# The first block of a convolution and MLP kernel: taps of two channel thirds on TensorE, zero products in front, loads reordered

## The chip, the cores and the metric

One core of one Trainium2 chip runs the whole program. The metric is the device time of one execution in microseconds, as the median of several executions; profiles come from the hardware profiler. Engines: PE is TensorE (PEld its weight loads), DVE is VectorE, ACT is ScalarE, POOL is GpSimd, SP is SyncE, which here only issues DMA transfers.

## The reference

```python
# x: (8, 4096, 192), weight: (8 heads, 7 taps), w_in: (192, 2048), w_out: (2048, 192)
w = softmax(weight, axis=-1)                      # 7 taps for each group of 24 channels
out[b, s, c] = sum(w[head(c), k] * x_pad[b, s + k, c] for k in range(7))   # causal, 6 zeros in front
h = out.reshape(32768, 192) @ w_in
return (h * sigmoid(h)) @ w_out                   # (32768, 192)
```

The weights come as 64-bit floats; the kernel makes 32-bit floats of them on the chip, with integer operations ("rounding").

## The kernel before

The kernel works through 32 blocks of 1024 tokens. A block is laid out as two halves of 512 tokens: channels are cut into three thirds of 64, and a tile has the 64 channels of the first half in partitions 0 to 63 and those of the second half in partitions 64 to 127. From the second block on, everything is pipelined by a hand-made plan and PE never pauses. The first block is special: it has to wait for loads, taps and rounded weights. These are its parts:

```python
def turn_in(b, k):                 # third k of x: transpose on DVE, nat -> xt (6 columns of pad in front)
    nc.vector.transpose(xt[:, k, pad : pad + TB], nats[b][:, k])

def conv(b, k, i):                 # tap i of third k; result in place of nat
    if i == 0 and b < 2:           # first tap on ACT
        nc.scalar.activation(dst, src, AF.Copy, scale=tap)
    ...
    else:                          # taps 1..6 on DVE: dst = src * tap + dst
        nc.vector.scalar_tensor_tensor(out=dst, in0=src, scalar=tap, in1=dst, op0=ALU.mult, op1=ALU.add)

def spread(b, k):                  # copy each half's 64 rows into both partition halves, by DMA
    for n in range(2):
        for e in range(2):
            nc.sync.dma_start(out=dups[b][R * e : R * e + R, n, k, :], in_=src[R * n : R * n + R, :])

def round_in(j, k=None):           # 64-bit words of w_in -> wr[j]: 8 to 10 operations on DVE and ACT
    ...

def up_plain(b, j):                # h = out @ w_in for 1/4 of the hidden units: 24 products of 64 rows, then SiLU
    ...                            # 8 PSUM banks; for j = 0 in the order of the thirds

for k in range(NK):                # the front of the first block
    if k == 0:
        turn_in(0, 0)
        conv(0, 0, 0)
    for i in range(1, K):
        conv(0, k, i)
    spread(0, k)
    if k < NK - 1:
        for j in ((1, 2), (3,))[k]:
            load_in(j, nc.sync)    # raw 64-bit weights
        turn_in(0, k + 1)
        conv(0, k + 1, 0)
    round_in(0, k)
round_in(1)
for j in range(NJ):
    up_plain(0, j)
    ...                            # rounding of the other weights
```

Each product of 32-bit floats is two instructions on PE. Products are written into the 8 PSUM banks (`ps` in the views); `bank()` takes one of them. `pin` keeps an instruction in program order. SiLU is h * sigmoid(h). In what follows, "j=1" is the second call of `up_plain`: 48 instructions, followed by 96 for j=2 and j=3.

Of the kernel before, what the change touches and what calls it, by code (L numbers as in the profile page):

```python
# [9 lines left out]
F32 = mybir.dt.float32  # L10
I32 = mybir.dt.int32
AF = mybir.ActivationFunctionType
ALU = mybir.AluOpType
# [4 lines left out]
def kernel(  # L18
# [24 lines left out]
    nc = tc.nc  # L43
# [3 lines left out]
    H, K = weight.shape  # L47
    NT = B * S
    DFF = moe_w_in.shape[1]
    P = 128  # L50
    R = 64
    NK = D // R
    grp = D // H
    pad = K - 1
    TB = 512
# [14 lines left out]
    xpool = ctx.enter_context(tc.tile_pool(name="xp", bufs=1))  # L70
    tpool = ctx.enter_context(tc.tile_pool(name="tp", bufs=3))
    gpool = ctx.enter_context(tc.tile_pool(name="gp", bufs=2 * NJ))
    upool = ctx.enter_context(tc.tile_pool(name="up", bufs=13))
# [29 lines left out]
    def pin(ins):  # L103
        return tc.keep_in_program_order(ins)
# [8 lines left out]
    vec, act = Pinned(nc.vector), Pinned(nc.scalar)  # L113

    def bank():
        return psum.tile([P, TB], F32, tag="ps", name="ps")

    nats, xts, gs = {}, {}, {}

    def load(b, ks=range(NK)):  # L120
        if b not in nats:
            nats[b] = xpool.tile([P, NK, TB // SQ, SQ], F32, tag="nat", name="nat")
        nat = nats[b]
        for k in ks:
            for i in range(P // SQ):
                c = R * k + SQ * (i % 2)
                (nc.sync if b or k or i % 2 else nc.scalar).dma_start(  # L127
                    out=nat[SQ * i : SQ * i + SQ, k, :, :],
                    in_=x_v[2 * b + i // 2][:, :, c : c + SQ],
                )  # L130


    wexp = const.tile([P, H, K], F32, name="wexp")
    nc.scalar.dma_start(
        out=wexp.rearrange("p h k -> p (h k)"),
        in_=weight.rearrange("(o h) k -> o (h k)", o=1).to_broadcast([P, H * K]),
# [5 lines left out]
    for k in range(NK):  # L142
        nc.gpsimd.dma_start(
            out=xts[0][R:P, k, 0:pad], in_=x0[:, k, :], allow_slow_non_contiguous=True
        )
    load(0, (0,))

    warm = const.tile([P, 1], F32, name="warm")
    vec.memset(warm, 0.0)
    act.activation(warm, warm, AF.Exp)  # L150


    WC = 2 * NK * P
# [2 lines left out]
    wr = [const.tile([P, 2, NK, P], F32, name=f"wr{j}") for j in range(NJ)]  # L156
# [5 lines left out]
    def raw_tile(key):  # L162

        pool, tag = (gpool, "g") if key in (("i", 2), ("i", 3)) else (tpool, "t")
        raws[key] = pool.tile([P, 4 * TB], I32, tag=tag, name="raw")[:, 0 : 2 * WC]
        return raws[key]

    def load_in(j, queue):
        raw = raw_tile(("i", j)).rearrange("p (a k c) -> p a k c", a=2, k=NK)
        for e in range(2):  # L170
            for a in range(2):
                c = 2 * P * (NM * a + 2 * j + e)
                queue.dma_start(
                    out=raw[R * e : R * e + R, a, :, :], in_=in32[:, :, c : c + 2 * P]
                )
# [53 lines left out]
    def round_in(j, k=None):  # L229

        words = raws["i", j].rearrange("p (a k c t) -> p a k c t", a=2, k=NK, t=2)
        if k is None:
            rounded(
                wr[j].rearrange("p a k c -> p a (k c)"),
                words.rearrange("p a k c t -> p a (k c) t"),
                j < 2,
            )
        else:
            rounded(wr[j][:, :, k, :], words[:, :, k], j < 2)
        if k in (None, NK - 1):  # L240

            del raws["i", j]
            for e in range(2):
                nc.gpsimd.dma_start(
                    out=ws[j][R * e : R * e + R], in_=wr[j][R - R * e : 2 * R - R * e]
                )
# [33 lines left out]
        comb(a_(1, 0), a_(0, 0), a_(1, 0), ALU.subtract)  # L280

    load_in(0, nc.sync)
    load(0, (1, 2))


    hot = const.tile([P, NK, H], F32, name="hot")
    nc.gpsimd.memset(hot, 1.0)
    for e in range(2):
        half = hot[R * e : R * e + R]
        for sign, base in ((1, 0), (-1, grp - 1)):  # L290
            nc.gpsimd.affine_select(
                out=half,
                in_=half,
                compare_op=ALU.is_ge,
                fill=0.0,
                base=base,
                pattern=[[sign * R, NK], [-sign * grp, H]],
                channel_multiplier=sign,
            )
    wred = const.tile([P, H], F32, name="wred")  # L300
    taps = const.tile([P, NK, K], F32, name="taps")
    each = const.tile([P, NK, K, H], F32, name="each")

    def per_head(t):
        return t.unsqueeze(2).to_broadcast([P, H, K])

    vec.tensor_reduce(wred, wexp, axis=AX.X, op=ALU.max)
    vec.tensor_tensor(wexp, wexp, per_head(wred), op=ALU.subtract)
    act.activation(wexp, wexp, AF.Exp)
    vec.tensor_reduce(wred, wexp, axis=AX.X, op=ALU.add)  # L310
    vec.tensor_scalar(wred, wred, scalar1=1e-9, scalar2=None, op0=ALU.add)
    vec.reciprocal(wred, wred)
# [12 lines left out]
    def turn_in(b, k):  # L325
        if k == 0 and b:
            xt = xts[b] = xpool.tile([P, NK, pad + TB], F32, tag="xt", name="xt")
            if b * TT % S == 0:
                nc.gpsimd.memset(xt[0:R, :, 0:pad], 0.0)
            else:  # L330
                nc.gpsimd.tensor_copy(xt[0:R, :, 0:pad], tails.pop(b))
        xt = xts[b]
        pin(
            nc.vector.transpose(  # L334
                xt[:, k, pad : pad + TB], nats[b][:, k, :, :].rearrange("p k c -> p (k c)")
            )
        )
        if k == NK - 1:
            if b:
                nc.sync.dma_start(out=xt[R:P, :, 0:pad], in_=xt[0:R, :, TB : TB + pad])  # L340
            if (b + 1) * TT % S:
                tails[b + 1] = xpool.tile([R, NK, pad], F32, tag="tail", name="tail", bufs=2)
                nc.sync.dma_start(out=tails[b + 1], in_=xt[R:P, :, TB : TB + pad])

    def conv(b, k, i):

        src = xts[b][:, k, i : i + TB]
        dst = nats[b][:, k, :, :].rearrange("p k c -> p (k c)")
        tap = taps[:, k, i : i + 1]
        if i == 0 and b < 2:  # L350
            pin(nc.scalar.activation(dst, src, AF.Copy, scale=tap))  # L351
        elif i == 0:
            pin(nc.vector.tensor_scalar(dst, src, scalar1=tap, scalar2=None, op0=ALU.mult))
        else:
            pin(
                nc.vector.scalar_tensor_tensor(  # L356
                    out=dst, in0=src, scalar=tap, in1=dst, op0=ALU.mult, op1=ALU.add
                )
            )

    def spread(b, k):

        if k == 0:
            dups[b] = xpool.tile([P, 2, NK, TB], F32, tag="dup", name="dup")
        src = nats[b][:, k, :, :].rearrange("p k c -> p (k c)")
        for n in range(2):
            for e in range(2):
                nc.sync.dma_start(
                    out=dups[b][R * e : R * e + R, n, k, :], in_=src[R * n : R * n + R, :]
                )  # L370

    dups, wins = {}, {}
# [15 lines left out]
    def rows(t, e):  # L388
        return t[R * e : R * e + R]

    def g_tile(b, j, a):
        if (b, j, a) not in gs:
            gs[b, j, a] = gpool.tile([P, 2, 2, TB], F32, tag="g", name="g")
        return gs[b, j, a]

    def up_plain(b, j):

        d = dups[b]
        outs = [(a, n) for a in range(2) for n in range(2)]
        hs = {(a, n, e): bank() for a, n in outs for e in range(2)}  # L400
        order = [(k, o) for k in range(NK) for o in outs]
        if j:
            order = [(k, o) for o in outs for k in range(NK)]
        for k, (a, n) in order:
            for e in range(2):
                nc.tensor.matmul(  # L406
                    hs[a, n, e],
                    rows(wr[j], e)[:, a, k, :],
                    rows(d, e)[:, n, k, :],
                    start=k == 0,  # L410
                    stop=k == NK - 1,
                )
            if k == NK - 1:
                for e in range(2):
                    g = g_tile(b, j, a)
                    act.activation(g[:, n, e, :], hs[a, n, e], AF.Silu)
# [229 lines left out]
    def begin_down(b):  # L646
        did.add((b, "down"))
        for k in range(NK):
            if b + 1 < NB and (b, f"v.{k}{K - 1}") in did:
                spread(b + 1, k)  # L650
# [82 lines left out]
            store(2, cols)  # L733


    for k in range(NK):
        if k == 0:
            turn_in(0, 0)
            conv(0, 0, 0)
        for i in range(1, K):  # L740
            conv(0, k, i)
        spread(0, k)
        if k < NK - 1:
            for j in ((1, 2), (3,))[k]:
                load_in(j, nc.sync)
            turn_in(0, k + 1)
            conv(0, k + 1, 0)
        round_in(0, k)
    round_in(1)
    for j in range(NJ):  # L750
        up_plain(0, j)
# [71 lines left out]
```

## Time and profile before

| | before |
|---|---|
| median, lowest to highest, us | 2418.23, 2418.12 to 2418.29 (3 runs) |
| span of the profile, us | 2416.3 |
| PE busy | 2388.7 us (99%), 17808 instructions |
| DVE busy | 2073.4 us (86%) |
| start of j=1, after PE's last wait | 37.67 us |

A busy share of 99% doesn't say where the other 1% is. The timeline of PE does: a line of it gives start, duration, engine, source line, operation, tiles and count, and in brackets how long the engine stood idle before and what released it. The prediction shows these lines and reads them.

### The profile page before, as it was taken

Reading aid. Unit: us, or ns where it says so; the run is one execution under the profiler, and the core shown is the slowest. Engines: PE = TensorE matmul, PEld = TensorE weight load, DVE = VectorE, ACT = ScalarE, POOL = GpSimd, SP = SyncE. Lnnn points to the kernel's source line nnn. Section 1 sums busy time; section 2 is a strip of 40 time slices with the busy share of each in tenths; the row PEclk is TensorE's granted clock in tenths of the full one; section 3 lists DMA queues with packets and bytes.
Section 4 is the critical chain, followed back from the end, with each engine's and each line's share of the span. In section 5 each row is a group of like instructions: output and inputs, shape, how many; then the busy total and the mean of one; then the engine's idle time right before and its main releaser. Section 6 shows DMA issues by size and latency. Waiting matters only on the chain.

```text
span 2416.3 us, 43191 instructions
## 1 busy us (share of the span) xinstructions
PE 2388.7 (99%) x17808; PEld 939.4 (39%) x17808; DVE 2073.4 (86%) x2823; ACT 989.4 (41%) x1856; POOL 68.2 (3%) x96
## 2 busy tenths in 40 slices
PE   6999999999999999999999999999999999999998
PEld 3334433334433344333443333443334433334333
DVE  8889888898888888888988889888888888898876
ACT  3234533345433345333454334543334533345432
POOL 3300000000000000000000000000000000000000
PEclk9999999999999999999999999999999999999999
DMA  8321222222222212222222222122221222222220
GB/s 157 75 45 37 39 45 53 43 43 39 36 53 50 43 32 40 50 53 40 40 36 44 53 44 47 35 36 53 53 41 34 42 45 54 41 40 43 38 40 14
DMA packets 454085, 111.65 MB, mean 46 GB/s; under 512 B 423936, under 2 KB 429056, under 8 KB 453888
## 3 DMA queue, kind: packets, MB, share of 16 engines
q1 hardware_dynamic: 450064, 106.89, 23.8%
q8 instruction: 139, 2.28, 0.4%
q0 software_dynamic: 480, 1.58, 0.3%
q10 hardware_dynamic: 3344, 0.42, 0.1%
q14 instruction: 58, 0.48, 0.1%
HBM read 31.49 MB, written 25.17 MB: 23 GB/s over the span
## 4 chain that ended last, share of the span: by engine, by line
PE 98%; DVE 1%; DMA 0%; ACT 0%; SPq 0%; issue 0%; ACTq 0%; DVEq 0%
PE ps L442 49%; PE ps L515 46%; PE ps L544 2%; PE ps L406 1%; DMA nat<-in_x_dram 0%; DVE nat L356 0%; DMA tail<-xt 0%; SPq L127 0%; DVE two L111 0%; ACT two L111 0%; ACT g L111 0%; DVE cmb L111 0%; DVE xt L334 0%; ACT u L111 0%; ACT nat L351 0%
## 5 line engine op out<-in xcount | busy, mean ns | idle before, releaser
L442 PE MATMUL ps<-dup,ws 64*128 64x512 f32 x2480 | 869.9, 589 | 0.0
L515 PE MATMUL ps<-g,wo 128*32 128x512 f32 x2976 | 661.8, 593 | 0.0
L466 DVE TENSOR_TENSOR g<-u,ps 128x512 f32<-128x512 f32 x744 | 485.5, 679 | 119.2 <-PE ps L442 90.0
L442 PE MATMUL ps<-win,wr 64*128 64x512 f32 x1488 | 567.7, 589 | 0.0
L515 PE MATMUL ps<-t,wo 128*32 128x128 f32 (+2 forms) x4528 | 500.6, 446 | 0.0
L463 ACT ACTIVATE g<-g 128x512 f32<-128x512 f32 x744 | 444.6, 631 | 97.3 <-DVE g L466 97.3
L442 PEld LDWEIGHTS ps<-dup,ws 64*128 64x128 f32 x2480 | 363.0, 187 | 292.0 <-issue 277.9
L515 PE MATMUL ps<-t,wx 128*32 128x512 f32 x2976 | 452.7, 592 | 0.0
L356 DVE SCALAR_TENSOR_TENSOR nat<-xt,taps,nat 128x512 f32<-128x512 f32 x576 | 432.0, 750 | 18.7 <-ACT nat L351 3.8
L442 PE MATMUL ps<-dup,wr 64*128 64x512 f32 x992 | 419.9, 596 | 0.0
L457 ACT COPY u<-ps 128x512 f32<-128x512 f32 x496 | 277.8, 588 | 229.1 <-PE ps L442 226.1
L583 ACT COPY cmb<-ps 96x512 f32<-96x512 f32 x30 | 17.4, 581 | 805.5 <-PE ps L515 805.5
L483 DVE TENSOR_TENSOR t<-g 128x1024 f32<-128x1024 f32 x248 | 299.6, 1219 | 27.3 <-PE ps L515 27.3
L483 DVE TENSOR_TENSOR t<-g,t 128x1024 f32<-128x1024 f32 x248 | 303.3, 1223 | 13.6 <-PE ps L515 3.2
L442 PEld LDWEIGHTS ps<-win,wr 64*128 64x128 f32 x1488 | 233.4, 187 | 175.5 <-issue 147.2
L515 PEld LDWEIGHTS ps<-t,wo 128*32 128x32 f32 x4528 | 180.3, 110 | 219.8 <-issue 199.5
L442 PE MATMUL ps<-win,ws 64*128 64x512 f32 x496 | 242.2, 589 | 0.0
L515 PE MATMUL ps<-g,wx 128*32 128x512 f32 x1488 | 234.5, 592 | 0.0
L515 PEld LDWEIGHTS ps<-t,wx 128*32 128x32 f32 x2976 | 121.9, 110 | 278.8 <-issue 269.5
L595 DVE TENSOR_TENSOR cmb<-cmb,ps 96x512 f32<-96x512 f32 x150 | 102.3, 682 | 135.2 <-ACT u L580 133.1
L442 PEld LDWEIGHTS ps<-dup,wr 64*128 64x128 f32 x992 | 160.5, 187 | 128.2 <-issue 114.3
L515 PEld LDWEIGHTS ps<-g,wo 128*32 128x32 f32 x2976 | 168.5, 110 | 98.3 <-issue 98.3
(59 smaller groups left out, 1205.4 us busy)
## 6 DMA issues: line engine op xcount, KB each, us to landing
dup<-nat SPq DMA_DIRECT2D x384, 128.0 KB, 2.3
nat<-in_x_dram SPq DMA_DIRECT2D x382, 64.0 KB, 2.4
out_dram<-osb SPq DMA_DIRECT2D x376, 64.0 KB, 2.0
raw<-in_moe_w_in_dram SPq DMA_DIRECT2D x16, 192.0 KB, 5.6
raw<-in_moe_w_out_dram SPq DMA_DIRECT2D x8, 384.0 KB, 3.9
ws<-wr POOLq DMA_DIRECT2D x8, 192.0 KB, 3.2
xt<-xt SPq DMA_DIRECT2D x31, 4.5 KB, 1.9
tail<-xt SPq DMA_DIRECT2D x24, 4.5 KB, 1.9
```

Of the source, the lines that this page charges most:

```text
L356: nc.vector.scalar_tensor_tensor(out=dst, in0=src, scalar=tap, in1=dst, op0=ALU.mult, op1=ALU.add)
L406: nc.tensor.matmul(hs[a, n, e], rows(wr[j], e)[:, a, k, :], rows(d, e)[:, n, k, :], start=k == 0, stop=k == NK - 1,)
L442: nc.tensor.matmul(bk[b, m, bn], rows(w, half), rows(v, half), start=first, stop=True, skip_group_check=True,)
L457: pin(copy(u, bk[b, m, "1"]))
L463: pin(nc.scalar.activation(g, g, AF.Silu))
L466: pin(nc.vector.tensor_tensor(g, us.pop((b, m, i)), bk[b, m, bn], op=ALU.add))
L483: pin(nc.vector.tensor_tensor(t[i // 2][:, i % 2, :], u, v, op=ALU.subtract))
L515: nc.tensor.matmul(accs[b][at][SQ * q : SQ * q + SQ, to], lhs[:, e, SQ * k : SQ * k + SQ], rhs[:, e, ts(q, TB // 4) if i == 5 else to], st ...
L544: nc.tensor.matmul(acc[k][R * n : R * n + R, :], wo[j][:, a, e, R * k : R * k + R], gs[b, j, a][:, n, e, :], start=j == 0 and a == 0 and e ...
L583: pin(nc.scalar.copy(c[0], acc[0][0:n, :]))
L595: pin(nc.vector.tensor_tensor(out_, u, v, op=ALU.add))
```

## The change

The intent is to take two of the three thirds' taps off DVE and give them to PE, which idles before j=1. A tap is a product with a diagonal matrix that holds the tap of each channel. Written as a 64x128 matrix with the diagonal twice, the product writes its result into both partition halves, so the copies by DMA (`spread`) go too. Four products of zeros in front are to raise PE's clock in time. The loads of the first block are kept in program order, with one of them on ACT's queue. The core of the diff, with cuts marked:

```diff
-                (nc.sync if b or k or i % 2 else nc.scalar).dma_start(
+                queue = nc.scalar if not b and (k == 0 and i % 2 == 0 or k == 1 and i == 0) else nc.sync
+                ins = queue.dma_start(
...
+                if not b:
+                    pin(ins)
...
+    zeros = upool.tile([P, TB], F32, tag="u", name="zeros")
+    vec.memset(zeros, 0.0)
+    idle = bank()
+    for _ in range(4):
+        pin(nc.tensor.matmul(idle, zeros[:, 0:P], zeros, start=True, stop=True))
...
     load_in(0, nc.sync)
-    load(0, (1, 2))
...
     act.activation(wexp, wexp, AF.Exp)
+    load(0, (1, 2))
...
-    for k in range(NK):
-        ...                                   (the loop shown above)
+    def diagonal(k):
+        for i in range(K):
+            act.activation(diag[:, k, i, :], one_hot, AF.Copy, scale=taps[:, k, i : i + 1])
+
+    def conv_pe(k):
+        by_pe[k] = [bank() for _ in range(2)]
+        for i in range(K):
+            for n in range(2):
+                pin(nc.tensor.matmul(by_pe[k][n], rows(diag, n)[:, k, i, :],
+                                     rows(xts[0], n)[:, k, i : i + TB], start=i == 0, stop=i == K - 1))
+
+    turn_in(0, 0)
+    diagonal(0)
+    conv_pe(0)
+    round_in(0, 0)
+    diagonal(1)
+    turn_in(0, 1)
+    conv_pe(1)
+    for j in (1, 2):
+        load_in(j, nc.sync)
+    turn_in(0, 2)
+    conv(0, 2, 0)
+    for n in range(2):
+        act.copy(dups[0][:, n, 0, :], by_pe[0][n])
+    for i in range(1, K):
+        conv(0, 2, i)
+    spread(0, 2)
+    load_in(3, nc.sync)
+    round_in(0, 1)
+    for n in range(2):
+        act.copy(dups[0][:, n, 1, :], by_pe[1][n])
+    round_in(0, 2)
     round_in(1)
```

POOL makes `one_hot`, the double identity, in five more instructions.

More of the change, by code (lines that the diff above doesn't have):

```diff
@@ L299 @@
             )
+    one_hot = upool.tile([P, TB], F32, tag="u", name="one_hot")[:, 0:P]
+    nc.gpsimd.memset(one_hot, 1.0)
+    for e in range(2):
+        half = one_hot[R * e : R * e + R].rearrange("p (a c) -> p a c", a=2)
+        for sign in (1, -1):
+            nc.gpsimd.affine_select(
+                out=half,
+                in_=half,
+                compare_op=ALU.is_ge,
+                fill=0.0,
+                base=0,
+                pattern=[[0, 2], [-sign, R]],
+                channel_multiplier=sign,
+            )
     wred = const.tile([P, H], F32, name="wred")
@@ L361, in spread @@
     def spread(b, k):
-        if k == 0:
+        if b not in dups:
             dups[b] = xpool.tile([P, 2, NK, TB], F32, tag="dup", name="dup")
@@ L405, in up_plain @@
             for e in range(2):
-                nc.tensor.matmul(
-                    hs[a, n, e],
-                    rows(wr[j], e)[:, a, k, :],
-                    rows(d, e)[:, n, k, :],
-                    start=k == 0,
-                    stop=k == NK - 1,
+                pin(
+                    nc.tensor.matmul(
+                        hs[a, n, e],
+                        rows(wr[j], e)[:, a, k, :],
+                        rows(d, e)[:, n, k, :],
+                        start=k == 0,
+                        stop=k == NK - 1,
+                    )
                 )
@@ L733, in finish @@
             store(2, cols)
-    for k in range(NK):
-        if k == 0:
-            turn_in(0, 0)
-            conv(0, 0, 0)
-        for i in range(1, K):
-            conv(0, k, i)
-        spread(0, k)
-        if k < NK - 1:
-            for j in ((1, 2), (3,))[k]:
-                load_in(j, nc.sync)
-            turn_in(0, k + 1)
-            conv(0, k + 1, 0)
-        round_in(0, k)
+    diag = gpool.tile([P, NK - 1, K, P], F32, tag="g", name="diag")
+    dups[0] = xpool.tile([P, 2, NK, TB], F32, tag="dup", name="dup")
+    by_pe = {}
+    def diagonal(k):
[5 more added lines that the diff above has]
+            for n in range(2):
+                pin(
+                    nc.tensor.matmul(
+                        by_pe[k][n],
+                        rows(diag, n)[:, k, i, :],
+                        rows(xts[0], n)[:, k, i : i + TB],
+                        start=i == 0,
+                        stop=i == K - 1,
+                    )
+                )
+    turn_in(0, 0)
[19 more added lines that the diff above has]
+    round_in(0, 2)
     round_in(1)
```

## The prediction

> **What bounds the kernel now.** I read the page first. Its strip of 40 slices shows PE at 9 in every slice but the first, at a granted clock of 9 tenths throughout. The chain that ended last is 98% PE.
>
> ```profile
> PE 2388.7 (99%) x17808; PEld 939.4 (39%) x17808; DVE 2073.4 (86%) x2823; ACT 989.4 (41%) x1856; POOL 68.2 (3%) x96
> ...
> PE   6999999999999999999999999999999999999998
> ...
> PE 98%; DVE 1%; DMA 0%; ACT 0%; SPq 0%; issue 0%; ACTq 0%; DVEq 0%
> ```
>
> The reader is to see that 2416.3 - 2388.7 = 27.6 us is all the idle time PE has, and that it can only lie at the front. So I asked for the timeline of PE, and for the chain in order of time.
>
> ```profile
> 16.59 6.29 PE L406 MATMUL ps<-dup,wr 64*128 64x512 f32 x16 [16.59 <-DVE wr L111]
> 27.01 10.15 PE L406 MATMUL ps<-dup,wr 64*128 64x512 f32 x32 [4.14 <-DMA dup<-nat]
> 37.67 31.17 PE L406 MATMUL ps<-dup,wr 64*128 64x512 f32 x144 [0.51 <-ACT g L111]
> ```
>
> ```profile
> 37.64 0.03 issue
> 37.67 31.17 PE ps L406 x144
> 68.84 41.35 PE ps L544 x192
> ```
>
> From 37.67 us on, PE never waits again for anything of weight: 16.6 + 4.1 + 0.5 = 21.2 us of its 27.6 us idle lie before. The time of the kernel is thus **37.7 us of front plus 2378.6 us of gapless PE**. Only the moment at which the second group of weights (j=1, 144 instructions for j=1 to 3) can start matters. The DVE timeline tells what sets it.
>
> ```profile
> 6.90 0.70 DVE L334 STREAM_TRANSPOSE xt<-nat 128x512 f32<-128x512 f32 x1
> 8.45 4.69 DVE L356 SCALAR_TENSOR_TENSOR nat<-xt,taps,nat 128x512 f32<-128x512 f32 x6 [0.84 <-ACT nat L351]
> 13.05 0.70 DVE L334 STREAM_TRANSPOSE xt<-nat 128x512 f32<-128x512 f32 x1
> 13.68 0.45 DVE L111 TENSOR_SCALAR two<-raw 128x256 int32<-128x256 int32 x2
> ...
> 16.45 4.68 DVE L356 SCALAR_TENSOR_TENSOR nat<-xt,taps,nat 128x512 f32<-128x512 f32 x6
> ...
> 24.45 4.68 DVE L356 SCALAR_TENSOR_TENSOR nat<-xt,taps,nat 128x512 f32<-128x512 f32 x6
> 29.05 0.49 DVE L111 TENSOR_SCALAR two<-raw 128x256 int32<-128x256 int32 x2
> ...
> 31.62 1.02 DVE L111 TENSOR_SCALAR two<-raw 128x768 int32<-128x768 int32 x2
> ...
> 36.43 1.09 DVE L111 SCALAR_TENSOR_TENSOR wr<-mh,two 128x768 f32<-128x768 f32 x1
> ```
>
> DVE works without a pause from 8.45 to 37.52 us: three thirds of taps (6 x 0.767 = 4.60 us each from start to start), three transposes, three roundings of the weights of j=0, one rounding of j=1. The last line ends at 36.43 + 1.09 = 37.52 us and writes the weights that j=1 reads; PE starts 0.15 us later. **DVE bounds the front, PE all the rest.**
>
> **What the Trainium skill says.** (1) "TensorE: Matmul & The Clock Gate", Part 1: the array runs at half clock until a free-running window of about 3.4 us has been busy, and falls back after an idle one. The trace agrees: the granted clock is 0.50 in the window of 27 to 28 us, at the start of a burst at 27.01, and full from about 32.0 us, 5.0 us later; the pitch of PE's pairs is 0.85 us before and 0.43 us after. (2) The same page, Part 3: matmuls on different row groups run at the same time. The trace agrees: two 64-row instructions of about 590 ns each retire every 0.43 us. (3) "FP8 and Floating Point Precision", TensorE Precision Notes: a true FP32 product takes four passes. The trace has two instructions for each matmul of the program, at 0.43 us for a pair of halves, so 0.86 us for two matmuls of 512 columns. (4) "DMA: Bandwidth & Descriptors", Queues, rings and completion order: an engine serves its queues in turn, packet by packet. So a load moved to the ACT queue gets ahead of SP's backlog and takes share from it; the trace before can't show that for this load.
>
> **The change, part by part.**
>
> Removed: on DVE 12 of the 18 tap instructions of the first block, 2 x 4.60 = 9.2 us. On ACT two of three first taps (0.72 us each). On SP eight of the twelve copies dup<-nat, about 2.4 us of issue per third and some 2 to 3 us to landing.
>
> Added on PE: 4 matmuls of zeros = 8 instructions, at 0.85 us cold and 0.43 us warm; started at about 1.4 us (after the memset, DVE's first work being at 0.89) they end between 6.5 and 8.2 us, depending on when the clock rises. Then per third 7 taps x 2 halves = 14 matmuls = 28 instructions, two at a time: 14 x 0.43 = 6.0 us, 12 us for both. They write both partition halves, so no dup copies are needed.
>
> Added on ACT: 14 diagonals of 128x128. ACT durations here are 0.20 us for 1 column, 0.25 for 56, 0.40 for 256, 0.72 for 512, so I estimate 0.3 us, 2.1 us per third. The first is ready soon after the taps (6.99 us), and PE eats one per 0.86 us, so they don't hold it. Four copies out of PSUM of 0.59 us each. On POOL the one-hot mask: four selects of 0.23 us grow to perhaps 0.4 us, ending at about 6.9 us, just in time.
>
> Moved: rounding of the first third of j=0 comes right after the first transpose on DVE, and taps remain only for the third third. DVE's order is now: transpose 0, round (0,0), transpose 1, transpose 2, taps of third 2, round (0,1), round (0,2), round j=1. I walk along it:
> - Transpose 0 at 6.90, as before, ended 7.6. Round (0,0) needs the raw weights. The last of their four loads was issued at 4.26 us:
>
> ```profile
> raw<-in_moe_w_in_dram SPq DMA_DIRECT2D x1, 192.0 KB, 6.5
> ```
>
>  so it landed at 10.76 us. That was hidden before (first used at 13.68) and isn't now. With a little lost to the load on the ACT queue I take 11.0. **DVE idles 3.4 us.**
> - Round (0,0): 2.57 us (as 29.05 to 31.62, without a wait for ACT), to 13.6. Transposes at 0.63 us pitch: transpose 2 starts at 14.2. Its data is the last of x to land; before, the next to last landed at 10.78 + 2.23 = 13.01, so it should be there.
> - First tap on ACT and the handover: 1.55 us from transpose to DVE's first tap (6.90 to 8.45): 15.75. Taps 4.60: 20.35. Round (0,1) 2.57: 22.9. Round (0,2) 2.57: 25.5. Round j=1 31.62 to 37.52 = 5.9: **31.4 us**.
>
> PE in parallel: taps 0 from about 7.7 or 8.2 to 14.2; taps 1 from 14.3 (transposed third at about 14.25) to 20.3; products of j=0, third 0, 8 pair slots = 3.4 us, its last two banks being freed by the copies of taps 1, which ACT makes behind the work for round (0,1), at about 22.8: done at 23.6; thirds 1 and 2 (weights at 22.9 and 25.5) 6.9 us: 30.5. ACT then has the j=1 rounding (to about 28.1), the table load of 1.28 us and SiLU from about 29.4, so banks are free in time. PE is ready about 1 us before DVE's weights. Start of j=1: about 31.5 instead of 37.67, **6.1 us earlier**.
>
> Behind it, DVE's rounding of j=2, j=3 and the output weights is one chain with the same durations, so it moves along by the same 6.1 us, and the waits of PE on it remain covered as before (weights of j=2 at 45.6 for a need at about 48). 2418.2 - 6.1 = **2412.1 us**.
>
> **Rivals.**
> (a) All 9.2 us arrive: 2409. Against it: the raw weights at 10.8 and the x loads at 13 us are walls that the order of DVE now runs into. If the raw loads land at 10 instead of 11, I get 2411.
> (b) PE becomes the bound of the front. If zeros don't warm the clock, or it drops again in a gap, the first taps run at 0.85 us a pair for some 3.4 to 5 us, and PE's slack of 1 us turns into 1 to 2 us lost: j=1 starts at 32.5 to 33.5, 2413 to 2414. For it: the first burst before ran 5.2 us at half pace. Against: the zeros come from 1.4 us on, long enough for a whole window.
> (c) Loads: if the reordered x and weight loads delay the raw weights to 13 us, DVE loses 2 us more: 2414. Total bytes up to there don't change, and the strip of DMA is nearly full from 4 to 10 us, so a shift to one side is possible.
> (d) Nothing is gained since the front was hidden: excluded by PE's 21.2 us idle before 37.67 us. A loss of 2% would be 48 us, more than the whole front.
>
> **Range and chances.** 2412.1 us from the walk; (a) gives the low end 2409.8, (b) and (c) together the high end 2415.2. All of this is 0.1 to 0.4% of the time, so within 2% is all but sure.
>
> **What would show it.** Right: a DVE timeline with idle time before the first rounding, released by the raw loads at about 11 us; six tap instructions left before 40 us; PE busy from about 1.5 us, full clock by 8.2 us; PE's last start after a wait at about 31.5 us with DVE's j=1 weights as releaser; from there to the end 2378.6 us as before. Wrong: if PE waits there for something else (ACT's SiLU, banks), if the clock is 0.5 during the tap matmuls, if the raw weights land elsewhere than 10 to 12 us, or if the stretch behind the front changes its length, for example because diag takes a g buffer and later tiles wait for it.

## The result, and the profile after

| | before | after |
|---|---|---|
| median of 6 runs each, us | 2418.11 | 2411.68 |
| lowest to highest, us | 2417.96 to 2418.29 | 2411.53 to 2412.07 |
| span of the profile, us | 2416.3 | 2410.0 |
| DVE's weights of j=1 ready, us | 37.52 | 31.23 |
| start of j=1, us | 37.67 | 31.38 |
| from there to PE's last end, us | 2372.29 | 2372.29 |
| from PE's last end to the end of the span, us | 6.36 | 6.29 |

The kernel is 6.43 us faster. The ratio is 0.9974 (95% interval 0.9961 to 0.9986): a small change, but the interval leaves out 1. Of the 6.43 us, the profile has 6.29 in the front. The long middle has the same length to a hundredth.

The timeline of PE in the changed kernel:

```profile
1.57 5.81 PE L159 MATMUL ps<-zeros 128*128 128x512 f32 x8 [1.57 <-DVE zeros L111]
8.04 12.59 PE L776 MATMUL ps<-xt,diag 64*128 64x512 f32 x56 [0.67 <-DVE xt L358]
20.44 10.50 PE L431 MATMUL ps<-dup,wr 64*128 64x512 f32 x48
31.38 31.17 PE L431 MATMUL ps<-dup,wr 64*128 64x512 f32 x144 [0.44 <-DVE wr L111]
```

PE now works from 1.57 us on. The taps of two thirds (56 instructions) took 12.59 us, and the 48 instructions of j=0 follow without a gap, at full clock. Then PE waits 0.44 us for DVE's rounded weights, its last wait; the 31.17 us of the 144 instructions behind it are those of before. The timeline of DVE:

```profile
7.20 0.70 DVE L358 STREAM_TRANSPOSE xt<-nat 128x512 f32<-128x512 f32 x1
10.93 0.49 DVE L111 TENSOR_SCALAR two<-raw 128x256 int32<-128x256 int32 x2 [3.03 <-DMA nat<-in_x_dram]
...
13.51 1.30 DVE L358 STREAM_TRANSPOSE xt<-nat 128x512 f32<-128x512 f32 x2
15.59 4.69 DVE L380 SCALAR_TENSOR_TENSOR nat<-xt,taps,nat 128x512 f32<-128x512 f32 x6 [0.79 <-ACT nat L375]
20.20 0.49 DVE L111 TENSOR_SCALAR two<-raw 128x256 int32<-128x256 int32 x2
...
30.27 0.96 DVE L111 SCALAR_TENSOR_TENSOR wr<-mh,two 128x768 f32<-128x768 f32 x1
```

DVE stands idle for 3.03 us before its first rounding: the raw weights aren't there yet. The bracket blames a load of x (`nat`), though the instruction reads `raw`. The chain of waits of the same kernel names the load of the weights:

```profile
5.18 5.67 DMA raw<-in_moe_w_in_dram
...
10.93 0.51 DVE two L111 x2
```

It was issued at 5.18 us and landed at 10.85, 5.67 us later. Where two views differ in the releaser, the operand that the instruction reads decides; loads of both kinds landed around that time.

The same care is due with PE's line of the kernel before, whose bracket at 37.67 us names ACT's SiLU (`g`) and not DVE's weights. In the eight runs in which PE waits before j=1 (before, after, e2, e3, e6, e8, e11, e12), j=1 starts 0.15 us after DVE's weights, whichever of the two is named. In the kernel before, the fourth SiLU ended just ahead of PE's start, at 37.63 us; in the changed kernel the fourth ended at 31.48, after PE had started at 31.38. So PE doesn't wait for that one, and the weights are what ends the wait.

DVE's budget closes with these lines. Before, it started its first taps at 8.45 us and needed 29.07 us to the weights of j=1. Now it starts its first rounding at 10.93 and needs 20.30. That is 8.77 us shorter and 2.48 us later, 6.29 us in all.

### The profile page after: what moved, and what is told of

It is laid out like the page before. It is cut to its first block, busy times and chain, and to the rows that moved or that the text cites. A ratio compares the mean times of both kernels' runs of the same rounds, so it can differ in the third digit from the quotient of the medians. Undisturbed runs are those within 1.5% of the kernel's fastest.

```text
span 2410.0 us, 43319 instructions
## 1 busy us (share of the span) xinstructions
PE 2401.0 (100%) x17872; PEld 943.9 (39%) x17872; DVE 2063.0 (86%) x2812; ACT 995.0 (41%) x1872; POOL 72.6 (3%) x101
## 4 chain that ended last, share of the span: by engine, by line
PE 98%; DVE 1%; DMA 0%; ACT 0%; issue 0%; SPq 0%; ACTq 0%; DVEq 0%
PE ps L468 49%; PE ps L541 47%; PE ps L570 2%; PE ps L431 1%; DVE two L111 0%; DMA raw<-in_moe_w_in_dram 0%; DVE nat L380 0%; DMA wexp<-in_weight_dram 0%; DVE mh L111 0%; DVE cmb L111 0%; DVE wr L111 0%; ACT two L111 0%; ACT u L111 0%; DVE osb L111 0%; DVE xt L358 0%
## 5 line engine op out<-in xcount | busy, mean ns | idle before, releaser
L380 DVE SCALAR_TENSOR_TENSOR nat<-xt,taps,nat 128x512 f32<-128x512 f32 x564 | 423.5, 751 | 18.3 <-ACT nat L375 3.7
```

## The experiments

Times differ by fractions of a microsecond here, so each run was read in the trace first: by the start of j=1 and by PE's last end. In every run below, 2372.2 to 2372.5 us lie between the two. What comes behind PE's last end, the final stores, took 5.88 to 7.53 us from run to run. So the measured times are blunter than the trace, by up to about a microsecond. There is one profile for each kernel; how much of the spread of the other timed runs lies there isn't shown.

| run | start of j=1 | DVE's weights of j=1 | behind PE's end | median time |
|---|---|---|---|---|
| before | 37.67 | 37.52 | 6.36 | 2418.11 |
| after | 31.38 | 31.23 | 6.29 | 2411.68 |
| e1_no_zeros | 31.75 | 31.26 | 6.29 | 2412.47 |
| e2_loads_only | 38.10 | 37.95 | 5.88 | 2417.51 |
| e3_pe_short | 31.43 | 31.28 | 6.29 | 2412.79 |
| e4_dve_short | 30.90 | 29.58 | 7.25 | 2412.02 |
| e5_both_short | 29.86 | 28.87 | 7.30 | 2411.16 |
| e6_one_third | 35.09 | 34.95 | 7.03 | 2416.36 |
| e7_three_thirds | 36.71 | 32.42 | 6.07 | 2416.98 |
| e8_hide_tap | 31.55 | 31.41 | 6.33 | 2412.05 |
| e9_early_weights | 37.04 | 35.74 | 5.96 | 2416.96 |
| e10_shared_third | 37.07 | 35.76 | 5.90 | 2416.42 |
| e11_kept_warm | 29.05 | 28.91 | 7.53 | 2410.24 |
| e12_zeros_only | 37.74 | 37.59 | 6.39 | 2418.29 |

The runs were made in three sessions; the kernel before had medians of 2418.18, 2418.21 and 2418.09 us in them. Theory: two chains run side by side in the front, DVE's to the weights of j=1 and PE's through taps and j=0, and the later one sets the time. Rivals: the loads or the zeros made the gain; DVE alone counts; PE alone counts.

### Shorter work on one chain, on the other, on both

e3 (wrong result): PE does four of the seven taps.

```diff
-        for i in range(K):
+        for i in range(0, K, 2):
             for n in range(2):
                 pin(nc.tensor.matmul(by_pe[k][n], ...
```

> Wrong result on purpose: PE does only taps 0, 2, 4, 6 of each third it has, 3 x 0.86 = 2.6 us less per third, 5.2 us less in all. DVE is as in the changed kernel. Theory (DVE's chain to the weights of j=1 bounds the front): j=1 still starts at 31.2 to 31.4, 2411.5 to 2411.8. Rival (PE's chain bounds): j=1 up to 5 us earlier, 2406.5.

```profile
14.41 5.40 PE L776 MATMUL ps<-xt,diag 64*128 64x512 f32 x16 [2.97 <-ACT diag L111]
31.43 31.17 PE L431 MATMUL ps<-dup,wr 64*128 64x512 f32 x144 [0.92 <-DVE wr L111]
```

Measured: j=1 at 31.43, DVE's weights at 31.28. PE had 5.2 us less to do and gained nothing by it. **DVE's chain bounds the changed kernel's front.** The test is milder than its edit looks: PE had to wait 2.97 us for the second group's diagonals and then ran it slowly (see e5), so it ended j=0 at 30.50 us instead of 30.94, only 0.44 us earlier. PE's wait for the weights grew by about as much, to 0.92 us, and j=1 didn't move with PE. The median of 2412.79 us is even higher; the trace shows no change of the front that would explain it, and its profiled run took 2411.95.

e4 (wrong): DVE does three instead of six taps of the last third.

```diff
-    for i in range(1, K):
+    for i in range(2, K, 2):
         conv(0, 2, i)
```

> Wrong result on purpose: DVE does three instead of six tap instructions of the third that it kept, 3 x 0.767 = 2.3 us less. PE is as in the changed kernel. Theory: DVE's weights of j=1 come at 28.9 us, but PE ends j=0 only at 30.9, so PE takes over as the bound and only 0.3 to 0.45 us are gained: j=1 at about 30.95, 2411.2. Rival (only DVE matters): all 2.3 us, j=1 at 29.1, 2409.4.

```profile
20.60 41.40 PE L431 MATMUL ps<-dup,wr 64*128 64x512 f32 x192
```

Measured: weights at 29.58, j=1 at 30.90 with PE working without a wait before it. DVE came 1.65 us earlier, not 2.3: its rounding of the last third waited 0.64 us for a step on ACT, which stood behind the copies of PE's second group of taps, so the two chains are not quite independent. Of the 1.65 us, 0.48 arrived at the start of j=1. So PE's chain stands right behind DVE's, as the trace of the changed kernel says by its wait of 0.44 us. The time doesn't show it: in the profiled run the stores behind PE's end took 7.25 us, 0.96 us more than in the changed kernel.

e5 (wrong): both edits.

> Wrong result on purpose: both shortenings at once. Theory: with PE out of the way DVE's 2.3 us come through whole: j=1 at about 29.1, 2409.4. If something third (loads, ACT's SiLU, banks) stands right behind both, less than 1 us is gained over the changed kernel: 2410.7 or more.

Measured: weights at 28.87, but j=1 only at 29.86: 1.52 us gained of 2.3. The expectation missed, and neither chain as I had drawn it explains it. The timeline of PE in this run tells why:

```profile
7.75 3.70 PE L776 MATMUL ps<-xt,diag 64*128 64x512 f32 x16 [0.53 <-DVE xt L358]
14.36 5.40 PE L776 MATMUL ps<-xt,diag 64*128 64x512 f32 x16 [2.90 <-ACT diag L111]
19.56 41.40 PE L431 MATMUL ps<-dup,wr 64*128 64x512 f32 x192
```

The same 16 instructions took 3.70 us the first time and 5.40 the second. Between them PE idled for 2.90 us. The view of stretches has the granted clock behind the busy times (it is the last number but two):

```profile
14.40:15.70 1.30, 1.30 (x6) 0.70 (x8) 0.51 (x2) 0.84 (x2) 0.00 (x0) 1.00 1.10 214
15.80:19.10 3.30, 3.30 (x11) 1.49 (x9) 3.15 (x8) 1.58 (x4) 0.00 (x0) 0.50 1.13 205
```

The clock fell to 0.50 at 15.8 us, 1.4 us after PE had gone back to work, and stayed there to 19.2. From 14.36 us on PE has no wait, so here it was the slowed PE that bounded. So e11 fills the gap with three more products of zeros.

```diff
     turn_in(0, 1)
+    idle2 = bank()
+    for _ in range(3):
+        pin(nc.tensor.matmul(idle2, zeros[:, 0:P], zeros, start=True, stop=True))
     conv_pe(1)
```

> Wrong result on purpose. Both shortenings at once, as before, with three products of zeros (2.6 us) in the gap of 2.9 us that let PE's clock fall to 0.5 from 15.8 to 19.2 us. Theory (the cold clock ate what was missing): clock 1.0 throughout, PE's second tap group 3.4 to 3.7 us instead of 5.4, DVE's weights bound again: j=1 at about 29.0 instead of 29.86. Rival (something else holds PE): j=1 at 29.8 again.

```profile
14.40 3.70 PE L776 MATMUL ps<-xt,diag 64*128 64x512 f32 x16
17.93 10.47 PE L431 MATMUL ps<-dup,wr 64*128 64x512 f32 x48
29.05 31.17 PE L431 MATMUL ps<-dup,wr 64*128 64x512 f32 x144 [0.65 <-DVE wr L111]
```

Measured: 3.70 us for the second group, and j=1 at 29.05 with DVE's weights as the releaser. All 2.33 us of DVE's saving arrive. The cold clock was what was missing in e5.

### The parts other than the taps

e2: the kernel before with the changed loads alone (of the diff above, the lines of the queue, `pin(ins)` and the moved `load(0, (1, 2))`).

> The kernel before with nothing but the changed loads of the first block (pinned order, one load of the second third on the ACT queue, issued behind the first activation). Theory: DVE bounds the front, and its first taps cover these loads, so the weights of j=1 still come at 37.5 us and j=1 starts at 37.7: 2418.2, no gain (within 0.4). Rival: the loads are where the gain is: up to several us faster, j=1 well before 37 us.

Measured: j=1 at 38.10, 0.43 us later than before. In the profiled run the stores at the end took 0.48 us less and made up for that: its span is 2416.3 us, as before. The median of the four timed runs was 0.7 us lower; no trace here shows why, as the profiled run was the slowest of them (2417.98). Nothing of the 6.3 us in the front comes from the loads.

e12: the kernel before with the four zero products alone.

> The kernel before with nothing but the four products of zeros in front. Theory: they warm a clock that falls again before the first real product at 16.6 us, and PE isn't the bound there: j=1 at 37.7, 2418.2, no gain. Rival (the zeros alone bring part of the gain): 1 us or more faster.

Measured: j=1 at 37.74; no gain. The clock was full from 5.36 us on, and back at 0.5 at 12.19, long before the first real product at 16.68.

e1: the changed kernel without the zero products.

```diff
-    for _ in range(4):
-        pin(nc.tensor.matmul(idle, zeros[:, 0:P], zeros, start=True, stop=True))
```

> The changed kernel without the four products of zeros. Theory: they only raise PE's clock before the first taps. Without them the taps start cold at about 8.0 us and run at half pace until a busy window has passed, 3.4 to 6.8 us of time, 1.7 to 3.4 us lost. PE was ready 0.3 us ahead of DVE's weights (30.94 against 31.23), so j=1 starts at about 32.7 to 34.4 instead of 31.38, and the time is 2413.0 to 2414.7. Rival: DVE alone bounds the front and a slower PE is hidden: 2411.7, j=1 at 31.4.

The timeline of PE in this run:

```profile
7.73 13.90 PE L773 MATMUL ps<-xt,diag 64*128 64x512 f32 x56 [7.73 <-DVE xt L355]
21.45 41.38 PE L428 MATMUL ps<-dup,wr 64*128 64x512 f32 x192
```

Measured: the taps took 13.90 us instead of 12.59, the clock rising at 11.0 us. No wait is left before j=1, so PE bounds, and j=1 starts at 31.75, 0.37 us later. I had expected 1.3 us or more. At half clock from 7.73 to 11.01 us PE loses half of 3.28 us, 1.64. Three small reserves absorb most of that: the taps started 0.31 us earlier in this run (7.73 against 8.04), the second group of taps no longer had to wait for its data, some 0.3 us, and PE's own wait before j=1, 0.44 us, is gone. The wait as the trace gives it runs from the end of the last product; that product takes 0.59 us, while the pitch of products is 0.43, so the next could have started about 0.16 us before that end. What is left by this sum is 0.4 us, near the 0.37 measured. The five timed runs lie between 2411.94 and 2413.29 us, a spread of 1.35 against 0.54 for the changed kernel. So the zeros are worth 0.4 us in the profiled run and 0.8 in the medians (in separate sessions). Whether they also steady the time isn't shown: e3, with the zeros and in the same session as e1, spreads by 1.18.

### Where the balance lies

e6: one third's taps on PE, two on DVE; the second third goes through `conv` and `spread` as the third does.

> The changed kernel with only the first third on TensorE; DVE does the taps of the second and the third. Theory: DVE's chain grows by one third's six tap instructions, 4.6 us, less about 0.6 us since the transpose of the last third now hides ACT's first tap: j=1 at 35.3 to 35.6 us, time 2415.6 to 416.0 (2415.6 to 2416.0). Rival (the loads or the early rounding made the gain, not the taps): stays near 2412.

Measured: j=1 at 35.09, a little earlier than expected, but 3.71 us later than with two thirds; the rival failed.

e7: all three on PE, with a `diagonal(2)`, a `conv_pe(2)` and two more copies in place of the taps and the spread.

> All three thirds on TensorE, no taps left on DVE in the first block. Theory: PE has no idle time left from 8.0 us on, so a further 6.0 us of tap matmuls come on top one for one, and what DVE saves is worth nothing: j=1 at about 37.0 us, time 2417.2 to 2417.6, nearly all of the gain given back. Rival (DVE still bounds): j=1 at about 26 to 27 us, 2407.

```profile
8.05 18.55 PE L778 MATMUL ps<-xt,diag 64*128 64x512 f32 x84
26.41 41.40 PE L431 MATMUL ps<-dup,wr 64*128 64x512 f32 x192
```

Measured: j=1 at 36.71, 5.33 us later than with two thirds, and PE has not one wait from 8.05 us on. Two thirds on PE is the best of the four splits: 37.67 with none, 35.09 with one, 31.38 with two, 36.71 with three (that with none is the kernel before; e2 and e12 show that its loads and missing zeros don't account for the difference). That isn't because taps are cheaper on PE. A third costs 6.0 us there and 4.6 on DVE; it is because PE had time to give up to that point and none beyond.

### Attempts at a better version

e8 puts `round_in(0, 1)` ahead of DVE's taps, to hide the 0.79 us for which DVE waits for ACT's first tap.

> The changed kernel with the rounding of the second third put ahead of the taps of the third third on DVE, so that ACT's first tap (DVE idle 0.79 us) is hidden. Correct result. Theory: DVE's weights of j=1 come 0.8 us earlier (30.4), but PE, ready at 30.94, bounds from there: j=1 at 30.9 to 31.0, 0.45 us gained, 2411.2. Rival: all 0.8 us, 2410.9; the two are apart in the trace, not in the time.

Measured: j=1 at 31.55, nothing gained. DVE's rounding needs a step on ACT, and that step now stands in ACT's queue behind the two copies out of PSUM. DVE waited 1.41 us there instead of 0.79:

```profile
16.88 0.42 DVE L111 SCALAR_TENSOR_TENSOR two<-raw,two 128x256 int32<-128x256 int32 x1 [1.41 <-ACT two L111]
```

e9 loads the weights of j=0 third by third, the first ahead of x's thirds two and three, and puts the copies behind the rounding; e10 gives two taps of the second third back to ACT and DVE on top of it. The core of e9:

```diff
-    load_in(0, nc.sync)
+    load_in(0, nc.sync, (0,))            # 4 loads of 64 KB: third 0 only
     ...
     load(0, (1, 2))
+    load_in(0, nc.sync, (1, 2))          # 8 loads of 64 KB
```

> Correct result. The changed kernel with the weights of j=0 loaded third by third, the first third (256 KB) ahead of the x loads of thirds two and three and the rest behind them, and with the rounding of the second third ahead of the last taps and ahead of the copies out of PSUM on ACT. Theory (DVE idles 3.0 us only because all 768 KB of weights have to land first): DVE's first rounding starts at 7.9 to 8.7 us instead of 10.9, its weights of j=1 come at 28 to 29 us instead of 31.2; but PE, gapless from 7.7 to 8.0 us on, then bounds: j=1 at 30.3 to 30.7, 0.7 to 1.1 us gained, about 2410.8. Rival (the x loads are a wall of their own right behind): weights of j=1 not before 30.5 us, under 0.4 us gained.

> Correct result. As the early weights, and two taps of the second third go back: the first to ACT, the second to DVE, their sum into PSUM by one more product with the double identity. PE has 0.86 us less, DVE 0.77 us more. Theory (two balanced chains): weights of j=1 at about 29.0, PE ready at about 29.5, j=1 at 29.4 to 29.9, 1.5 to 2.0 us gained over the changed kernel, about 2410. Rival: a wait of the extra product for DVE's part stops PE, and j=1 stays at 30.5 or later.

```profile
6.88 0.70 DVE L374 STREAM_TRANSPOSE xt<-nat 128x512 f32<-128x512 f32 x1
15.05 0.50 DVE L111 TENSOR_SCALAR two<-raw 128x256 int32<-128x256 int32 x2 [7.47 <-DMA raw<-in_moe_w_in_dram]
```

Both failed: j=1 at 37.04 and 37.07. The loads themselves did in e9 what was meant: the first third had landed at 7.71 us, and the last load of x at 10.51 instead of 13.41. Yet DVE's first rounding started only at 15.05. The trace has the eleventh of the twelve weight loads landing at 14.93 and the twelfth at 15.54. A third lies in the tile in two pieces, one in each half of it, with the other thirds in between; the eleventh load is the last that falls between the two pieces of the first third, and the twelfth lies behind them. So the likely reason is that the wait was made for the whole range from the first piece to the second. What the two runs show is what late weights cost. The first rounding came 4.1 us later than in the changed kernel, and DVE's weights of j=1 came 4.5 us later. PE's second group of taps was held up too, as its diagonals stand in ACT's queue behind the rounding's step; the clock fell to 0.5, and j=1 started 5.7 us late. Whether earlier weights would gain anything stays open. A version that beats the changed kernel with a correct result did not come of this.

## Why the prediction was right

The time was 2411.68 us against 2412.1 predicted, in the range of 2409.8 to 2415.2. Its steps, against the trace:

- **The whole gain lies ahead of PE's last wait, and the rest moves along unchanged.** Right: 2372.29 us from there to PE's last end in both kernels, and 2372.2 to 2372.5 in all experiments. A reading on the way was wrong: that PE's idle time "can only lie at the front". Of the 27.6 us, 6.4 lie behind PE's last end (the last slice of the strip is an 8, not a 9); they cancelled, as they hardly changed (6.36 and 6.29).
- **The wait for the raw weights comes into the open.** Right: predicted at 11.0 us, measured 10.93. This is the step that turns 9.2 us of removed DVE work into 6 us of gain. e9 and e10 show it from the other side.
- **DVE's walk.** Transposes, taps and roundings started within 0.3 us of the predicted times, as all durations came from rows of the trace before. The "without a pause" of that trace overlooks two waits for ACT of 0.32 and 0.31 us, each in a rounding; the sum rightly took the length of a rounding from the third one, which has no such wait. Weights of j=1: predicted 31.4, measured 31.23.
- **PE ready about 1 us ahead of DVE.** Only 0.44 us: PE ended j=0 at 30.94, not at 30.5. The second group of taps ended 0.1 us later than in the sum, and the products of j=0 took 10.50 us to the end of the last, not 10.2; the sum counted pitches of 0.43 us, and the last product runs 0.59. The conclusion held by a hair: e3 shows DVE as the bound, e4 PE 0.5 us behind it.
- **Rival (b), the cold clock.** The zeros did their work by 5.85 us, earlier than the latest time allowed for. Without them (e1) PE does become the bound, but it costs 0.4 us in the profiled run, less than the 1 to 2 that the prediction named.
- **Rival (c), loads that delay the weights, and a middle that changes its length:** neither happened. e2 shows that the loads alone bring nothing. The load moved to ACT's queue was issued at 5.05 us and landed at 10.07, between the weight loads issued at 4.54 and 5.18 (9.77 and 10.85): in order of issue, so that it got ahead of SP's backlog isn't seen here.
- **The clock falls back after an idle window.** Too simple: in e5 a gap of 2.90 us was enough, though the window that the prediction names is about 3.4 us. That the window runs freely fits the traces' clock records: between the first and the last change, each state lasts 3.41 us or a multiple of it (6.83, 10.24, 17.07 in the fronts of the runs).

## What to carry to other kernels

When an engine that is 99% busy has its idle time in one place, find the last wait there and walk the chain that ends in it; what is taken off that chain counts only until the next arrival (here a load that landed at 10.9 us) or the next chain (here PE, 0.44 us behind). Handing work to an idle engine pays up to the point where both chains end together, even if each piece costs more there, and turns into a loss one step beyond. For differences of a microsecond, compare the moments in the trace that your argument is about; the total carries the noise of the last stores.

## What the Trainium skill lacked or had wrong

- "TensorE: Matmul & The Clock Gate", "Why this matters for your kernels", advises no idle gaps over about 3 us between bursts. The runs put the figure a little lower: with gaps of 2.90 us in e5 and 2.97 in e3 and e6 the clock fell to 0.50, 0.7 to 1.4 us after work had resumed, and in e5 16 instructions took 5.40 us instead of 3.70; with a gap of 1.43 us in e6 it didn't fall. Nor does the page say that products of zeros count as activity: they do, the clock was full 4.3 us after the first of them in the changed kernel (3.0 to 5.9 us in the eleven runs that have them), and in e11 they held it at 1.0. And it warns that recorded clock events can't always be trusted, without this case: until the first event a trace shows 1.00, while weight loads of 0.34 us against 0.19 later show half speed (zeros before 5.85 us in the changed kernel).
- From PE's last end to the end of the span, 5.88 to 7.53 us passed for the same work in these runs.
